# The scale of an expert weight in three VectorE operations, its squares' sum read as bfloat16 without a cast

## The chip, the cores and the metric

The kernel runs on one core of a Trainium2 chip. The metric is the time of one execution on the device in microseconds (us). Engine names are those of the profile: PE is TensorE's matmul and PEld its weight load, DVE is VectorE, ACT is ScalarE, POOL is GpSimd, SP is SyncE, which here only issues transfers.

## The reference

Three layers follow one another. Top-32 attention (2 batches, 8 heads, 576 rows, head size 64) makes 1152 rows of 512 values. A gated mixture layer with root-mean-square norm maps them to 1152 rows of 512. The last layer sends each row to one of eight experts and is the one that the change touches:

```python
logits = x @ w_gate                       # 1152 x 8
expert_idx = np.argmax(logits, axis=1)
# ... gate_w: softmax probability of the chosen expert; disp[e]: its rows, in order, up to 288
h = np.maximum(np.einsum('ecd,edf->ecf', disp, w1), 0.0)     # w1: 8 x 512 x 1024
y = np.einsum('ecf,efd->ecd', h, w2)                         # w2: 8 x 1024 x 512
out[i] = gate_w[i] * y[expert_idx[i], pos[i]]
```

## The kernel before

The 1152 rows are worked on as nine tiles of 128 (`NT` = 9, tile numbers 0 to 8). Attention and the gated layer fill the first three quarters of the span; the code writes their steps as generators that are advanced slot by slot, and the order of the instructions on each engine is then fixed by a planner that simulates the program and takes ready instructions by priority (`tc.high_priority(offset=...)` raises one). `after(...)` adds an edge: what stands in its block is not issued ahead of the instruction named. Each engine and each transfer queue works in the order so planned.

The experts' sixteen weight matrices (w1 and w2 of eight experts, 2 MB each, eight blocks of 128 x 512 fp32) are loaded one after the other in `ORDER`; n is the place in that order, j = 2e + w the matrix (w is 0 for w1, 1 for w2). A matrix isn't multiplied in fp32. It is scaled by a power of two and split into two fp16 halves, and `product` (L921) multiplies high by high, high by low and low by high, three matmuls for each 128 x 128 block. For each matrix:

- `load` (L773) issues two transfers on SP into a landing buffer; four buffers are used in turn, so a load waits for the conversion of an earlier matrix.
- `size` (L784) squares the matrix on ACT, in four pieces for n below 4 and in two later (L795); each piece leaves one sum per partition in a column of the small tile `sc`.
- `scale` (L800) casts these sums to bfloat16 on DVE (L804), adds them over partitions with matmuls against a matrix of ones (`st`, L806), and makes the power of two from the total on DVE: times 1.01 plus a tiny number (L807), shift right and mask (L809), times -1 plus a constant (L810), exponent alone (L148 in `exponent`), and the inverse of the power (L151 in `invert`). For w2 a further operation multiplies the two inverses of the expert (L816).
- `convert` (L818) writes the high half, one half of it on ACT (L825) and the other on DVE (L827), and the low half on DVE (L830).

`up` (L928) multiplies the gathered rows by w1 and applies the ReLU (high half on ACT L936, low half on DVE L937); `down` (L939) and `finish` (L976) multiply by w2 and take the scales out again on DVE (L945, L981, L994); `send` (L962) transposes back, multiplies by the gate on ACT (L973) and scatters the rows with POOL.

The first four matrices are sized and converted while the last tile (tile 8) still passes through the gated layer, and their DVE and ACT work is mixed with that tile's: its tanh (ACT L510), the products with it (DVE L511 and L514, which must be done before PE can transpose the result, L486), and the halves for the next matmul (ACT L470, DVE L471, then PE L531). After L531 the tile goes through `dispatch` (L540): router, slot, and a scatter by POOL (L621). Only then are rows gathered (L841, L854, L908), and behind these gathers SP issues the next weight loads.

```python
    with after(NT - 1, "sq"):
        size(0, 0)
        size(1, 1)
    with after(NT - 1, "xn"), after(NT - 1, "xn high"):
        convert(0, 0)
    size(2, 2)
    ...
    with tc.issue_after(last.ins):
        for _ in range(3):
            fetch_w()
```

A second copy of the program, for more than 168 rows of one expert (`exact`), is in the code behind a condition and isn't executed with these inputs.

Of the kernel before, what the change touches and what calls it, by code (L numbers as in the profile page):

```python
# [8 lines left out]
F32 = mybir.dt.float32  # L9
F32R = mybir.dt.float32r  # L10
F16 = mybir.dt.float16
BF16 = mybir.dt.bfloat16
I32 = mybir.dt.int32
U32 = mybir.dt.uint32
U8 = mybir.dt.uint8
AF = mybir.ActivationFunctionType
OP = mybir.AluOpType
PSUM = bass.MemoryType.PSUM

P = 128  # L20
# [19 lines left out]
TINY = 1e-24  # L40
# [22 lines left out]
def whole(  # L63
# [3 lines left out]
    nc = tc.nc  # L67
# [10 lines left out]
    ones16 = const.tile([P, P], BF16, name="ones16")  # L78
# [68 lines left out]
    def exponent(out, x):  # L147
        nc.vector.tensor_scalar(out.bitcast(I32), x.bitcast(I32), 0x7f800000, None, op0=OP.bitwise_and)  # L148

    def invert(out, x):  # L150
        nc.vector.tensor_scalar(out.bitcast(I32), x.bitcast(I32), -1, 0x7f000000, op0=OP.mult, op1=OP.add)  # L151
# [108 lines left out]
    raw = {}  # L260
# [47 lines left out]
    hi, lo = {}, {}  # L308
# [164 lines left out]
    yx, late, behind = {}, [], {}  # L473

    def after(*what):

        return tc.issue_after(behind[what].ins)
# [62 lines left out]
    def dispatch(t):  # L540
# [11 lines left out]
        nc.scalar.activation(sq.bitcast(BF16), y, AF.Square, accum_out=yn[:, 0:1])  # L552
        size = iter(()) if t == NT - 1 else pow2_below_rsqrt(yn[:, 1:2], yn[:, 2:3], yn[:, 0:1], 1.01, yn[:, 3:5])
        next(size, None)
        yield
        lp = px.tile([P, 3, E], F32, name="px")
# [138 lines left out]
    for p in range(NP):  # L695
        t, hp = divmod(p, 4)
# [11 lines left out]
    for t in range(NT):  # L708
        ew = nc.vector if t in (0, 8) else nc.gpsimd
# [35 lines left out]
    ew = ctx.enter_context(tc.tile_pool(name="ew", bufs=1, reuse_waits="tile"))  # L745
# [5 lines left out]
    es = {}  # L751
# [11 lines left out]
    def place(j):  # L763
        x = slots[slot_of[j]].bitcast(F16)
        return x[:, :8 * DM], x[:, 8 * DM:]

    def raw_of(n):

        if n < 2:
            return slots[2 + n]  # L770
        return raws[n % 2 if n < 4 else n % 4]
# [10 lines left out]
    BIG = 4 * DM  # L782

    def size(j, n):  # L784

        e, w = divmod(j, 2)
        raw = raw_of(n)
        sc = ew.tile([P, 13], F32, name="sc", bufs=8)
        k = 4 if n < 4 or exact else 2
        for g in range(k):  # L790
            if exact:
                junk = mx.tile([P, DM], F32, name="th").bitcast(BF16)
            else:
                junk = ew.tile([P, BIG], BF16, name="junk")[:, :2 * BIG // k]
            nc.scalar.activation(junk, raw[:, g * 2 * BIG // k:(g + 1) * 2 * BIG // k], AF.Square, accum_out=sc[:, 9 + g:10 + g])  # L795
        with tc.high_priority(offset=4000) if n < 4 and not exact else nullcontext():
            scale(e, w, n, k, sc)
        sized[j] = sc

    def scale(e, w, n, k, sc):  # L800

        t = sums_of[:, n % 8:n % 8 + 1]
        s16 = ew.tile([P, 4], BF16, name="s16", bufs=2)
        nc.vector.tensor_copy(s16[:, :k], sc[:, 9:9 + k])  # L804
        for g in range(k):
            nc.tensor.matmul(t[:, 0:1], ones16, s16[:, g:g + 1], start=(g == 0), stop=(g == k - 1))  # L806
        nc.vector.tensor_scalar(sc[:, 2:3], t[:, 0:1], 1.01, TINY, op0=OP.mult, op1=OP.add)  # L807
        half_bits = sc[:, 3:4].bitcast(I32)
        nc.vector.tensor_scalar(half_bits, sc[:, 2:3].bitcast(I32), 1, 0x7fff0000, op0=OP.logical_shift_right, op1=OP.bitwise_and)  # L809
        nc.vector.tensor_scalar(half_bits, half_bits, -1, 0x5f370000 + ((10, 14)[w] << 23), op0=OP.mult, op1=OP.add)  # L810
        exponent(sc[:, 7:8], sc[:, 3:4])
        invert(sc[:, 4:5], sc[:, 7:8])
        if w == 0:
            es[e] = sc
        else:
            nc.vector.tensor_tensor(es[e][:, 8:9], es[e][:, 4:5], sc[:, 4:5], op=OP.mult)  # L816

    def convert(j, n, high=True, low=range(4)):  # L818

        raw, (hi, lo), sc = raw_of(n), place(j), sized[j]  # L820
        k = 4 if n < 4 else 2
        for g in range(k) if high else ():
            r = slice(g * 2 * BIG // k, (g + 1) * 2 * BIG // k)
            if 2 * g < k:
                nc.scalar.activation(hi[:, r], raw[:, r], AF.Copy, scale=sc[:, 7:8])  # L825
            else:
                nc.vector.tensor_scalar(hi[:, r], raw[:, r], sc[:, 7:8], None, op0=OP.mult)  # L827
        for g in low[:k]:
            r = slice(g * 2 * BIG // k, (g + 1) * 2 * BIG // k)
            nc.vector.scalar_tensor_tensor(lo[:, r], raw[:, r], sc[:, 7:8], hi[:, r], op0=OP.mult, op1=OP.subtract)  # L830

    meta, every, xgT, hE, yT2 = {}, {}, {}, {}, {}
    had = route.tile([P, 1], F32, name="had", bufs=1)
# [23 lines left out]
    def chunks(n):  # L857
        return [(o, min(P, n - o)) for o in range(0, n, P)]
# [17 lines left out]
# [6 lines that stand above are left out]
    with after(NT - 1, "xn"):  # L882
        convert(1, 1, True, (0, 1))
    with after(NT - 1, "gs", 0):
        convert(1, 1, False, (2, 3))
# [29 lines left out]
    def groups(count, n):  # L915

        pieces = -(-count // (DM // n))
        g = -(-count // pieces)
        return [(c, min(c + g, count)) for c in range(0, count, g)]

    def product(a, w, x, nk, width, col, of=None):  # L921
        wh, wl = (y.rearrange("p (c f) -> p c f", f=width) for y in w)
        for c in of or range(nk):
            for n, (u, v) in enumerate(((wh, x[0]), (wh, x[1]), (wl, x[0]))):
                nc.tensor.matmul(a, u[:, c, col * P:(col + 1) * P], v[:, c, :a.shape[-1]],  # L925
                                 start=(c == 0 and n == 0), stop=(c == nk - 1 and n == 2))
# [12 lines left out]
    def down(k, e, n):  # L939
        yT2[k] = eb.tile([P, KC, n], F32, name="yT2", bufs=1)  # L940
        for lo, hi in groups(KC, n):
            a = pacc.tile([P, hi - lo, n], F32, name="acc")
            for c in range(lo, hi):
                product(a[:, c - lo, :], place(2 * e + 1), hE[k], NF2, DM, c)
            behind[k, "down"] = nc.vector.tensor_scalar(yT2[k][:, lo:hi, :], a, es[e][:, 8:9], None, op0=OP.mult)  # L945

    targets = {}

# [27 lines left out]
    def finish():  # L976
        k, x, cut, y = E - 1, KC - 1, NF2 - 3, eb.tile([P, KC, W], F32, name="yT2", bufs=1)
        a, z = (pacc.tile([P, w, W], F32, name="acc") for w in (x, 1))
        for c in range(x):
            product(a[:, c, :], place(2 * k + 1), hE[k], NF2, DM, c)  # L980
        nc.vector.tensor_scalar(y[:, :x, :], a, es[k][:, 8:9], None, op0=OP.mult)  # L981
        product(z[:, 0, :], place(2 * k + 1), hE[k], NF2, DM, x, range(cut))
        for i, (o, m) in enumerate(chunks(W)):
            ob, to = held[0].tile([P, DM], F32, name=f"last{i}"), held[0].tile([P, 1], I32, name=f"to{i}")
            with after("b", "down"):
                nc.vector.tensor_copy(to[:m], every[i][:m, k, 1:2])
            held.append((to[:m], ob[:m], False))
            tp = pback.tile([P, DM], F32, name="back")
            for c in range(x):
                last = nc.tensor.transpose(tp[:m, c * P:(c + 1) * P], y[:, c, o:o + m], ident)  # L990
            scaled(i, ob[:m, :x * P], tp[:m, :x * P], meta[k, i][:m, 0:1])
        with tc.issue_after(last.ins):
            product(z[:, 0, :], place(2 * k + 1), hE[k], NF2, DM, x, range(cut, NF2))
        nc.vector.tensor_scalar(y[:, x:, :], z, es[k][:, 8:9], None, op0=OP.mult)  # L994
        for i, (o, m) in enumerate(chunks(W)):
            tp = ptp.tile([P, P], F32, name="col")
            nc.tensor.transpose(tp[:m], y[:, x, o:o + m], ident)
            scaled(i, held[1 + i][1][:, x * P:], tp[:m], meta[k, i][:m, 0:1])

    def scaled(i, out, x, by):  # L1000
        if i:
            nc.vector.tensor_scalar(out, x, by, None, op0=OP.mult)
        else:
            nc.scalar.activation(out, x, AF.Copy, scale=by)
# [23 lines left out]
    def ready():  # L1028
# [11 lines left out]
        fetch_w()  # L1040

    down("a", 0, WA)
    up("b", 0, WB)
    ready()
    send("a", WA, True)
    up(1, 1, W)
    ready()
    down("b", 0, WB)
    ready()
    cnt = pback.tile([P, DM], F32, name="back")  # L1050
# [23 lines left out]
    if not exact:  # L1074
        finish()
        return nc.values_load(top[0:1, 0:1], min_val=0, max_val=2 * N), held, store
# [59 lines left out]
```

## Time and profile before

| what | value |
|---|---|
| time, three runs | 661.33, 662.97, 663.25 us; median 662.97 |
| the profiled execution's own time | 663.15 us, of which 661.2 us are the span |
| busy share of the span | PE 89%, PEld 62%, DVE 82%, ACT 76%, POOL 54% |
| granted TensorE clock, mean | 0.976 of full speed |
| chain that ended last, by engine | PE 52%, DVE 17%, ACT 9%, DMA 8%, POOL 6%, issue 6% |

All times inside the trace count from the start of the span. The share of the span is an average over very different stages, so what a change in one stage is worth is read from that stage: which engine has no idle time there, and which wait ends last. The profiled execution took 663.15 us, 0.18 us more than the median.

### The profile page before, as it was taken

The page shows a single profiled execution, that of the slowest core. Times are in us where ns is not written, and L with a number is a line of the kernel's source. Part 1 is how long each engine was busy: PE and PEld are TensorE (multiplying, and loading weights), DVE is VectorE, ACT ScalarE, POOL GpSimd, SP SyncE. Part 2 cuts the span into 40 slices and gives each one's busy share as a digit, 9 for nine tenths or more (in the row PEclk, how much of TensorE's full clock was granted, in tenths as well). Part 3 has the DMA queues.
Part 4 walks back from the last instruction along what each step waited for, and adds up shares of the span by engine and source line. Part 5 has one row for each costly group of instructions (what it writes and reads, how often), then busy time and mean ns, then how long its engine had stood idle before and what let it go on. Part 6 is the DMA issues. An engine that isn't in the chain of part 4 may idle for free.

```text
span 661.2 us, 13479 instructions
## 1 busy us (share of the span) xinstructions
PE 588.5 (89%) x4817; PEld 412.1 (62%) x4817; DVE 540.5 (82%) x1495; ACT 502.3 (76%) x972; POOL 353.8 (54%) x490
## 2 busy tenths in 40 slices
PE   1418879799999999999999999999998888999995
PEld 1314455545666666666666666665544688999995
DVE  3989999978989979989988999871379756999961
ACT  3459978997787878878897988875697539999721
POOL 2486644646468879958788688583212200123212
PEclk9999979799999999999999999999999898999998
DMA  8998355923000010100000000007600499999001
GB/s 217 271 327 292 142 183 181 303 85 83 20 16 25 18 45 9 33 17 29 14 13 30 17 26 0 1 17 266 245 17 34 142 213 395 309 355 359 28 22 43
DMA packets 47008, 80.07 MB, mean 121 GB/s; under 512 B 18717, under 2 KB 23325, under 8 KB 46931
## 3 DMA queue, kind: packets, MB, share of 16 engines
q1 hardware_dynamic: 45138, 74.28, 35.7%
q0 software_dynamic: 1792, 4.83, 2.0%
q8 instruction: 40, 0.66, 0.4%
q14 instruction: 38, 0.30, 0.1%
HBM read 64.35 MB, written 12.27 MB: 116 GB/s over the span
## 4 chain that ended last, share of the span: by engine, by line
PE 52%; DVE 17%; ACT 9%; DMA 8%; POOL 6%; issue 6%; SPq 1%; POOLq 0%; DVEq 0%; ACTq 0%
PE pm L502 15%; PE pm L531 9%; PE acc L925 7%; PE xps L430 6%; PE tp L317 5%; PE tp L422 4%; DVE split L830 3%; DMA vt<-in_v_l_dram 3%; DMA raw<-in_w_dram 3%; ACT junk L795 2%; DVE r L373 2%; DVE wbig L169 2%; DVE wbig L168 2%; PE pm L486 2%; DVE split L827 2%
## 5 line engine op out<-in xcount | busy, mean ns | idle before, releaser
L502 PE MATMUL pm<-wbig,xn 128*128 128x512 f16 x600 | 145.7, 379 | 0.5 <-DVE hT L471 0.5
L925 PEld LDWEIGHTS <-split 128*128 128x128 f16 x1728 | 116.4, 99 | 4.3 <-issue 2.0
L399 POOL TENSOR_TENSOR pp<-s,pp 128x576 f32<-128x576 f32 x72 | 101.9, 1431 | 21.8 <-ACT pp L398 21.5
L502 PEld LDWEIGHTS <-xn 128*128 128x128 f16 x648 | 62.3, 98 | 60.2 <-issue 0.9
L376 DVE MAX8 m<-r 128x8 f32<-128x288 f32 x216 | 96.5, 452 | 2.5
L373 DVE MATCH_REPLACE8 r<-m,r 128x288 f32<-128x288 f32 x216 | 95.1, 442 | 0.0
L317 PE MATMUL tp<-kst,qh 128*128 128x288 f32 (+1 forms) x160 | 64.9, 413 | 31.9 <-ACT s L319 14.6
L531 PE MATMUL pm<-wbig,hT 128*128 128x512 f16 x324 | 78.4, 386 | 0.0
L830 DVE SCALAR_TENSOR_TENSOR split<-raw,sc,split 128x2048 f16<-128x2048 f32 (+1 forms) x32 | 65.9, 2077 | 0.5 <-ACT split L825 0.5
L319 ACT ACTIVATE s<-tp 128x288 f32<-128x288 f32 x144 | 56.7, 416 | 11.1 <-PE tp L317 9.5
L423 ACT ACTIVATE pt<-tp 128x384 f32<-128x384 f32 x108 | 51.8, 499 | 15.2 <-PE tp L422 10.6
L317 PEld LDWEIGHTS tp<-kst,qh 128*128 128x128 f32 (+1 forms) x160 | 31.4, 197 | 50.5 <-ACT s L319 20.7
L422 PE MATMUL tp<-ident,pp 128*128 128x128 f32 x324 | 57.8, 288 | 5.3 <-DVE r L325 2.5
L430 PE MATMUL xps<-pt,vt 128*64 128x128 f32 (+1 forms) x800 | 62.4, 275 | 0.0
L925 PE MATMUL acc<-hE,split 128*128 128x168 f16 (+2 forms) x864 | 59.9, 231 | 1.7 <-DVE hE L937 1.7
L795 ACT ACTIVATE junk<-raw 128x2048 bf16<-128x2048 f32 (+1 forms) x32 | 54.1, 1692 | 6.9 <-DMA raw<-in_w_dram 6.7
L398 ACT ACTIVATE pp<-s,bias 128x576 f32<-128x576 f32 x72 | 52.2, 777 | 9.4 <-POOL bias L381 9.3
L404 ACT ACTIVATE pp<-pp,bias 128x576 f32<-128x576 f32 x72 | 57.0, 792 | 2.3 <-POOL pp L399 2.1
L925 PE MATMUL acc<-xgT,split 128*128 128x168 f16 (+1 forms) x768 | 58.0, 239 | 0.0
L422 PEld LDWEIGHTS tp<-ident,pp 128*128 128x128 f32 x324 | 40.5, 145 | 23.8 <-ACT pt L423 3.8
L430 PEld LDWEIGHTS xps<-pt,vt 128*64 128x64 f32 x800 | 43.9, 139 | 13.7 <-issue 12.0
L531 PEld LDWEIGHTS <-hT 128*128 128x128 f16 x324 | 30.4, 99 | 33.5 <-issue 2.7
(241 smaller groups left out, 1227.7 us busy)
## 6 DMA issues: line engine op xcount, KB each, us to landing
raw<-in_w_dram SPq DMA_DIRECT2D x28, 1024.0 KB, 7.4
wbig<-in_w_gate_dram SPq DMA_DIRECT2D x6, 1024.0 KB, 8.5
wbig<-in_w_val_dram SPq DMA_DIRECT2D x6, 1024.0 KB, 8.3
wraw<-in_w_out_dram SPq DMA_DIRECT2D x12, 512.0 KB, 5.8
disp<-wraw SPq DMA_DIRECT2D x18, 257.0 KB, 6.5
qraw<-in_q_l_dram SPq DMA_DIRECT2D x72, 64.0 KB, 2.2
wbig<-in_k_l_dram SPq DMA_DIRECT2D x16, 288.0 KB, 4.4
split<-in_w_dram SPq DMA_DIRECT2D x4, 1024.0 KB, 9.3
```

The lines of the kernel that those rows point to most:

```text
L317: nc.tensor.matmul(sp[:c1], x[:, i, :c1], kst[b, hp][:, i, c * HALF:(c + 1) * HALF], start=(n == 0), stop=(n == 1))
L373: nc.vector.match_replace(h[i], to[n - 1][:, i], h[i], -3.0e38)
L376: nc.vector.max(to[n][:, i], h[i])
L399: nc.gpsimd.tensor_tensor(w, s[i], w, op=OP.subtract)
L404: nc.scalar.activation(pp[p][:, i], pp[p][:, i], AF.Exp, bias=bias[:, i, 0:1], scale=0.125, accum_out=sums[t][:, h:h + 1])
L422: nc.tensor.transpose(tp[:, i, :], p2[:, o:o + P], ident)
L430: nc.tensor.matmul(xps[t][rows, hp, c0:c1], v, w, start=(n == 0), stop=(n == 4))
L502: behind[t, "prod", b] = nc.tensor.matmul(a, xn[:, x + c, :], half(i, lo), start=(c == 0 and n == 0), stop=(c == KC - 1 and n == 2))
L531: nc.tensor.matmul(yps, hT[f // KC][:, KC * hi + f % KC, :], half(i, lo), start=(f == 0 and n == 0), stop=(f == NF1 - 1 and n == 2))
L795: nc.scalar.activation(junk, raw[:, g * 2 * BIG // k:(g + 1) * 2 * BIG // k], AF.Square, accum_out=sc[:, 9 + g:10 + g])
L830: nc.vector.scalar_tensor_tensor(lo[:, r], raw[:, r], sc[:, 7:8], hi[:, r], op0=OP.mult, op1=OP.subtract)
L925: nc.tensor.matmul(a, u[:, c, col * P:(col + 1) * P], v[:, c, :a.shape[-1]], start=(c == 0 and n == 0), stop=(c == nk - 1 and n == 2))
```

## The change

`scale` no longer casts the sums and no longer multiplies by 1.01. The matmul against ones reads the upper 16 bits of each fp32 sum in place, through a bfloat16 view with a step of two. Three DVE operations follow: shift right by one and mask to the exponent (reading the matmul's result in PSUM as integers), times -1 plus a constant (the power of two, column 1), plus a constant (its inverse, column 2). The tile `sc` shrinks from 13 to 7 columns and `s16` is gone. The product of the two inverses is not formed; the operations that take the scales out again get both inverses as per-partition scalars and multiply twice.

```diff
-        sc = ew.tile([P, 13], F32, name="sc", bufs=8)
+        sc = ew.tile([P, 7], F32, name="sc", bufs=8)
...
-            nc.scalar.activation(junk, raw[:, ...], AF.Square, accum_out=sc[:, 9 + g:10 + g])
+            nc.scalar.activation(junk, raw[:, ...], AF.Square, accum_out=sc[:, 3 + g:4 + g])
...
         t = sums_of[:, n % 8:n % 8 + 1]
-        s16 = ew.tile([P, 4], BF16, name="s16", bufs=2)
-        nc.vector.tensor_copy(s16[:, :k], sc[:, 9:9 + k])
+        high = sc.bitcast(BF16).rearrange("p (c two) -> p c two", two=2)[:, :, 1]
         for g in range(k):
-            nc.tensor.matmul(t[:, 0:1], ones16, s16[:, g:g + 1], start=(g == 0), stop=(g == k - 1))
-        nc.vector.tensor_scalar(sc[:, 2:3], t[:, 0:1], 1.01, TINY, op0=OP.mult, op1=OP.add)
-        half_bits = sc[:, 3:4].bitcast(I32)
-        nc.vector.tensor_scalar(half_bits, sc[:, 2:3].bitcast(I32), 1, 0x7fff0000, op0=OP.logical_shift_right, op1=OP.bitwise_and)
-        nc.vector.tensor_scalar(half_bits, half_bits, -1, 0x5f370000 + ((10, 14)[w] << 23), op0=OP.mult, op1=OP.add)
-        exponent(sc[:, 7:8], sc[:, 3:4])
-        invert(sc[:, 4:5], sc[:, 7:8])
-        if w == 0:
-            es[e] = sc
-        else:
-            nc.vector.tensor_tensor(es[e][:, 8:9], es[e][:, 4:5], sc[:, 4:5], op=OP.mult)
+            nc.tensor.matmul(t[:, 0:1], ones16, high[:, 3 + g:4 + g], start=(g == 0), stop=(g == k - 1))
+        root, by, back = (sc[:, i:i + 1].bitcast(I32) for i in range(3))
+        c = (11, 15)[w]
+        nc.vector.tensor_scalar(root, t.bitcast(I32), 1, 0x7f800000, op0=OP.logical_shift_right, op1=OP.bitwise_and)
+        nc.vector.tensor_scalar(by, root, -1, (189 + c) << 23, op0=OP.mult, op1=OP.add)
+        nc.vector.tensor_scalar(back, root, (65 - c) << 23, None, op0=OP.add)
+        es.setdefault(e, []).append(sc[:, 2:3])
...
-                nc.scalar.activation(hi[:, r], raw[:, r], AF.Copy, scale=sc[:, 7:8])
+                nc.scalar.activation(hi[:, r], raw[:, r], AF.Copy, scale=sc[:, 1:2])
...
-            behind[k, "down"] = nc.vector.tensor_scalar(yT2[k][:, lo:hi, :], a, es[e][:, 8:9], None, op0=OP.mult)
+            behind[k, "down"] = nc.vector.tensor_scalar(yT2[k][:, lo:hi, :], a, es[e][-2], es[e][-1], op0=OP.mult, op1=OP.mult)
```

L827 and L830 take their scale from column 1 in the same way as L825, and L981 and L994 take two scalars in the same way as L945.

## Rows read from the trace of the kernel before

**Rows 1.** Stages of the span's end: busy us (instructions) per engine, clock, DMA share, GB/s
```profile
485.40:510.10 24.70, 21.72 (x127) 11.40 (x126) 23.87 (x50) 21.64 (x38) 4.42 (x7) 1.00 0.00 1
...
538.00:549.90 11.90, 8.96 (x184) 8.81 (x179) 1.33 (x4) 5.35 (x7) 1.03 (x1) 1.00 1.03 354
...
560.00:622.00 62.00, 62.00 (x848) 61.50 (x846) 59.56 (x99) 58.16 (x64) 13.81 (x7) 1.00 0.92 287
622.00:623.30 1.30, 0.07 (x2) 0.05 (x1) 1.30 (x4) 0.97 (x2) 0.72 (x1) 1.00 0.00 0
```

**Rows 2.** Operations on the tile sc: line, engine, count, min/median/max ns
```profile
L804 DVE CAST s<-sc x16: 149/160/303, 481.6 to 619.4; 128x2 bf16<-128x2 f32 x12, 128x4 bf16<-128x4 f32 x4
...
L816 DVE TENSOR_TENSOR sc<-sc x8: 146/150/213, 496.4 to 632.5; 128x1 f32<-128x1 f32 x8
```

**Rows 3.** DVE in order of time, 485 to 510: start, us, line, operation [idle before]
```profile
485.65 0.16 DVE L807 TENSOR_SCALAR sc<-st 128x1 f32<-128x1 f32 x1 [0.55 <-PE st L806]
...
486.62 0.17 DVE L804 CAST s<-sc 128x4 bf16<-128x4 f32 x1 [0.25 <-ACT junk L795]
...
487.00 1.42 DVE L827 TENSOR_SCALAR split<-split,sc 128x1024 f16<-128x1024 f32 x2
...
493.11 0.15 DVE L807 TENSOR_SCALAR sc<-st 128x1 f32<-128x1 f32 x1
...
496.40 0.15 DVE L816 TENSOR_TENSOR sc<-sc 128x1 f32<-128x1 f32 x1
...
503.42 0.14 DVE L561 COPY lg<-px 128x8 f32<-128x8 f32 x1
503.49 0.13 DVE L810 TENSOR_SCALAR sc<-sc 128x1 int32<-128x1 int32 x1
...
509.25 0.73 DVE L514 SCALAR_TENSOR_TENSOR gs<-late,st,th 128x512 f32<-128x512 f32 x1
```

**Rows 4.** DVE in order of time: two scale operations back to back
```profile
531.31 0.15 DVE L809 TENSOR_SCALAR sc<-sc 128x1 int32<-128x1 int32 x1
531.50 0.15 DVE L810 TENSOR_SCALAR sc<-sc 128x1 int32<-128x1 int32 x1
```

**Rows 5.** PE in order of time, 501 to 511
```profile
501.44 0.95 PE L558 MATMUL px<-rg,xu 128*128 128x8 f32 x8
...
510.04 0.72 PE L486 MATMUL pm<-ident,gs 128*128 128x128 f32 x4 [1.82 <-DVE gs L514]
510.55 8.31 PE L531 MATMUL pm<-wbig,hT 128*128 128x512 f16 x30
```

**Rows 6.** ACT and PE in order of time around 549
```profile
542.42 4.51 PE L925 MATMUL acc<-xgT,split 128*128 128x168 f16 x60
549.43 0.19 ACT L795 ACTIVATION_READ_ACCUMULATOR junk<-raw 128x1 f32 x1
549.87 0.19 PE L806 MATMUL st<-s,ones 128*128 128x1 bf16 x2 [2.94 <-DVE s L804]
```

**Rows 7.** Matmuls over bfloat16 values at a step of two (line L193)
```profile
L193 PE MATMUL tp<-wbig x144: 217/219/331, 23.9 to 116.3; 128*128 128x128 bf16 x144
```

**Rows 8.** DVE operations without and with two per-partition scalars, and the last scaling
```profile
L603 DVE TENSOR_SCALAR pos<-k x1: 146/146/146, 523.9 to 523.9; 128x1 f32<-128x1 f32 x1
...
L619 DVE TENSOR_SCALAR slot<-pos x1: 274/274/274, 524.7 to 524.7; 128x1 int32<-128x1 f32 x1
...
653.73 0.39 DVE L994 TENSOR_SCALAR yT<-acc,sc 128x168 f32<-128x168 f32 x1
```

**Rows 9.** Stages as in rows 1, around pauses of PE; then PE after one pause
```profile
510.00:514.00 4.00, 3.96 (x13) 1.74 (x14) 3.80 (x13) 2.71 (x3) 2.63 (x4) 0.57 0.69 262
...
538.00:540.00 2.00, 2.00 (x86) 2.00 (x82) 0.59 (x2) 0.00 (x0) 0.00 (x0) 1.00 1.13 207
...
550.00:555.00 5.00, 5.00 (x117) 4.98 (x115) 4.80 (x14) 5.00 (x7) 0.00 (x0) 0.66 1.04 418
...
537.74 2.60 PE L925 MATMUL acc<-xbT,split 128*128 128x48 f16 x96 [1.68 <-DMA xbT<-xb]
```

More of the change, by code (lines that the diff above doesn't have):

```diff
@@ L794, in size @@
                 junk = ew.tile([P, BIG], BF16, name="junk")[:, :2 * BIG // k]
-            nc.scalar.activation(junk, raw[:, g * 2 * BIG // k:(g + 1) * 2 * BIG // k], AF.Square, accum_out=sc[:, 9 + g:10 + g])
+            nc.scalar.activation(junk, raw[:, g * 2 * BIG // k:(g + 1) * 2 * BIG // k], AF.Square, accum_out=sc[:, 3 + g:4 + g])
         with tc.high_priority(offset=4000) if n < 4 and not exact else nullcontext():
@@ L824, in convert @@
             if 2 * g < k:
-                nc.scalar.activation(hi[:, r], raw[:, r], AF.Copy, scale=sc[:, 7:8])
+                nc.scalar.activation(hi[:, r], raw[:, r], AF.Copy, scale=sc[:, 1:2])
             else:
-                nc.vector.tensor_scalar(hi[:, r], raw[:, r], sc[:, 7:8], None, op0=OP.mult)
+                nc.vector.tensor_scalar(hi[:, r], raw[:, r], sc[:, 1:2], None, op0=OP.mult)
         for g in low[:k]:
             r = slice(g * 2 * BIG // k, (g + 1) * 2 * BIG // k)
-            nc.vector.scalar_tensor_tensor(lo[:, r], raw[:, r], sc[:, 7:8], hi[:, r], op0=OP.mult, op1=OP.subtract)
+            nc.vector.scalar_tensor_tensor(lo[:, r], raw[:, r], sc[:, 1:2], hi[:, r], op0=OP.mult, op1=OP.subtract)
     meta, every, xgT, hE, yT2 = {}, {}, {}, {}, {}
@@ L980, in finish @@
             product(a[:, c, :], place(2 * k + 1), hE[k], NF2, DM, c)
-        nc.vector.tensor_scalar(y[:, :x, :], a, es[k][:, 8:9], None, op0=OP.mult)
+        nc.vector.tensor_scalar(y[:, :x, :], a, es[k][-2], es[k][-1], op0=OP.mult, op1=OP.mult)
         product(z[:, 0, :], place(2 * k + 1), hE[k], NF2, DM, x, range(cut))
@@ L993, in finish @@
             product(z[:, 0, :], place(2 * k + 1), hE[k], NF2, DM, x, range(cut, NF2))
-        nc.vector.tensor_scalar(y[:, x:, :], z, es[k][:, 8:9], None, op0=OP.mult)
+        nc.vector.tensor_scalar(y[:, x:, :], z, es[k][-2], es[k][-1], op0=OP.mult, op1=OP.mult)
         for i, (o, m) in enumerate(chunks(W)):
```

## The prediction

> **What bounds the kernel now.** I read the shares of busy time first, then the stages of the last third, then the engines in order of time there. The shares name PE, but the stages differ. From 560 to 622 PE is busy for all 62.00 us, DVE for 59.56 and ACT for 58.16 [rows 1]: PE sets the pace, and a DVE operation saved there buys slack only. The one pause that DVE makes for PE is 1.23 us at 622 to 623.3 [rows 1]; DVE is there behind a conversion that itself waited for ACT, and ACT's work isn't changed. From 485.4 to 510.1 it is the other way round: DVE is busy 23.87 of 24.70 us and PE 21.72 [rows 1], and the stretch ends with PE waiting 1.82 us for DVE's L514 [rows 5]. What DVE gains there moves the last tile's L531, its router and scatter, the gathers behind the scatter and the weight loads that SP issues behind the gathers, so it should move the end by the same amount. The reader is to see that of 16 scalings only the first four lie in a stretch where DVE is late.
>
> **The change part by part.** Each scaling loses the cast and goes from five small operations to three; the eight of w2 lose L816 too [rows 2]: 16 x 3 + 8 = 56 operations of some 0.15 us. What one costs in time is its step to the next start. Behind one another, each on the one before, they start 0.19 us apart (531.31 to 531.50) [rows 4]; between other work the step is 0.07 (493.11 to 493.18, 503.42 to 503.49) [rows 3].
>
> The Trainium skill, page "VectorE: DVE Perf Modes", section "The DRAIN you can't avoid", says that eight copies take the same time with a semaphore after each as with one after the last, so that a wait between neighbours adds nothing. The trace doesn't agree: a dependent neighbour starts 0.12 us later than an independent one. By the rule every operation that goes from the stage would count 0.07, and the ten of them with a stall of 0.25 us would give 0.95 and a time of 661.9.
>
> First matrix: L807 starts at 485.65 when the matmul is done, and the conversion (L827) at 487.00 [rows 3]. Between them stand five small operations and the cast of the second matrix, which sits in DVE's queue until ACT has finished that matrix's squares (0.25 us idle) [rows 3]. Afterwards there is no cast to wait in, and the conversion follows three operations: 0.19 + 0.19 + 0.07 = 0.45 us in place of 1.35. Gain 0.90.
>
> Second matrix: seven small operations from 493.11 to 496.40 [rows 3], steps 0.07 + 0.19 + 0.06 + 0.12 + 0.19 + 0.07 + 0.07 = 0.77. Three stay, at 0.07 + 0.19 + 0.06. Gain 0.45, so 1.35 by 503.42.
>
> There a bound comes in. The copy of the router's logits (L561, 503.42) needs PE's L558, which ends at 501.44 + 0.95 = 502.39 [rows 5], and PE's order up to it has no pause. With 0.06 us from one engine to the other (as from L514's end, 509.25 + 0.73, to PE at 510.04 [rows 3, 5]) the copy can't start before 502.45, so only 0.97 of the 1.35 is kept. Third matrix: four more small operations from 503.49 on [rows 3], 0.30 us, of which about 0.12 stays: gain 0.18. So L514 at 509.25 [rows 3] moves by 1.15 us, and PE's wait with it. The fourth matrix's operations lie beside the 8.31 us of L531 [rows 5] and cost nothing; without that cover they would be worth what the third's six are, some 0.3.
>
> At 549.87 PE stood 2.94 us in front of the sum for a later matrix, of which the cast is the last part: ACT's sums were out at 549.43 + 0.19 = 549.62 [rows 6]. PE now waits for ACT itself and, with 0.06 us between engines, can go on at 549.68. If the matmul keeps its place, that is 0.19 gained; behind it in PE's queue stand 11 matmuls and then the next group, which ACT and DVE evict. If it is planned earlier by the cast's length, three matmuls of some 0.07 us (4.51 / 60 [rows 6]) land behind it and the gain is nothing; I take 0.19, since the plan's order is likelier to stay than to shift by exactly that. PE shows no pause at any other sum.
>
> Two costs. The second scalar: an operation with two takes 0.274 us against 0.146 with none [rows 8]; one scalar was there already, so the price is between 0 and 0.13, and I take 0.07. Of 16 such operations only L994 [rows 8] is on the path to the end, since PE has other matmuls beside the others: 0.07 lost. The matmul over a step of two: the row with such a step shows 128 columns at 0.219 us [rows 7], and two of the one-column sums take 0.19 together [rows 6]; between 0 and 0.05 each, I take 0, with up to 0.2 on the first matrix's path. The add that makes the inverse isn't in the trace; its neighbours' steps are 0.06 to 0.19, and only the lower end stands in front of a conversion.
>
> Sum: 1.15 + 0.19 - 0.07 = 1.27 us. The profiled execution's 663.15 becomes 661.88; it lies 0.18 above the median, so 661.7 is forecast for the median. Its own range, from the bounds above (gain 0.6 without the second and third terms kept, 2.0 if the logits come early too), is 661.0 to 662.4.
>
> **Rivals.** *The clock stays up.* From 485.4 on PE pauses 24.70 - 21.72 = 2.98 us [rows 1], 1.82 of it just before 510 [rows 5] and 1.16 in front of the transposes before those. They were followed by a granted clock of 0.57 from 510 to 514, in the middle of L531 [rows 9]: between its levels of 1.2 and 2.4 GHz, a loss of 0.43 x 4 = 1.7 us on the path. With DVE earlier the first pause vanishes and one of about 1.8 remains. For it: after a lone pause of 1.68 us [rows 9] the clock was 1.00 [rows 9]. Against it: 2.94 us alone brought 0.66 [rows 6, 9], and 1.8 lies between. Time 661.7 - 1.7 = 660.0.
>
> *Nothing moves.* The planner puts a conversion or an ACT step ahead of the last tile's instead, or the gain of the front is given back where PE and the loads run at 1.03 of the DMA engines' share from 538 [rows 1]. For it: ACT too is busy 21.64 of 24.70 us [rows 1], and the planned order is remade. Time 663.0.
>
> *Slower: the sum blocks PE.* Without the cast the matmul is ready sooner in the plan and may be put ahead of the 60 matmuls at 542.42 [rows 6]. PE then stands from 542.4 to 549.65 and does 60 x 0.074 = 4.4 us of work after the wait that it now does before. Each matmul passed costs 0.074; from 17 on, the 1.27 is gone. At 60 the time is 661.7 + 4.4 = 666.1. For it: PE has stood there already, so the plan expects the load sooner than it lands. Against it: the cast is only 0.17 us long.
>
> That the change doesn't do what it says hardly comes into question: the count of operations is fixed by the code.
>
> **How the numbers follow.** Forecast 0.40, clock kept 0.27, a larger gain from a better order 0.06, nothing 0.14, slower 0.13. A measurement of this kernel tells about 0.3% (2.0 us) from no change: faster means under 661.0, slower over 665.0. Faster: 0.25 of the second case, 0.06, and 0.08 from the lower end of the first: 0.39. Slower 0.12; the rest, 0.49, is the same. A range of 659.3 to 664.3 leaves out most of the slower and the larger cases.
>
> **What would show it.** In the profile after: no cast; the first matrix's L827 about 0.45 us after its first scale operation; the pause before the transposes of L514's last product (510.04) about 1.15 us earlier; SP's first weight load behind the gathers earlier by the same; PE full from 550 to 620 as before. The forecast is wrong if that transpose comes at 510 again, if PE waits longer for a sum, or if the clock after it differs from 0.57.

## The result and the profile after

The changed kernel took 654.51 us (median of 4 runs, 653.21 to 655.98) beside 662.46 for the kernel before: a ratio of 0.9884 [0.986, 0.9908]. Later (h0 below) it took 656.6 (6 runs, 654.61 to 658.75) beside 661.89: 0.9912 [0.9881, 0.9944]. So it is 5 to 8 us faster, and 661.7 with a range down to 659.3 was wrong.

The profiled execution took 654.35 us (span 652.4). The stage that answers to [rows 1] is a little shorter, and PE's stage without a pause is as full as before. Windows of the changed kernel (length, then busy time of PE, PE's loads, DVE, ACT and POOL with instruction counts, granted clock, DMA share, GB/s):

```profile
483.90:506.50 22.60, 21.66 (x123) 11.32 (x121) 22.25 (x40) 21.68 (x37) 3.04 (x6) 1.00 0.07 19
...
510.00:514.00 4.00, 3.59 (x17) 1.44 (x15) 4.00 (x6) 0.37 (x1) 0.89 (x1) 1.00 0.39 114
...
532.00:534.00 2.00, 1.94 (x49) 1.94 (x50) 0.00 (x0) 0.00 (x0) 0.00 (x0) 0.51 1.13 205
...
552.00:612.50 60.50, 60.50 (x832) 60.28 (x830) 60.09 (x76) 59.08 (x65) 14.56 (x7) 1.00 0.99 314
```

The stretch to the last transposes is 22.60 us long where it was 24.70, and the clock in the block behind it is 1.00 where it was 0.57 [rows 9]. It falls to 0.51 at 532 instead. DVE in the front of the changed kernel (start, length, operation, idle time before it), against [rows 3]:

```profile
483.46 0.15 DVE L808 TENSOR_SCALAR sc<-st 128x1 int32<-128x1 int32 x1
483.65 0.15 DVE L809 TENSOR_SCALAR sc<-sc 128x1 int32<-128x1 int32 x1
483.72 0.14 DVE L810 TENSOR_SCALAR sc<-sc 128x1 int32<-128x1 int32 x1
484.05 1.42 DVE L822 TENSOR_SCALAR split<-split,sc 128x1024 f16<-128x1024 f32 x2 [0.19 <-DVE sc L810]
485.38 4.87 DVE L825 SCALAR_TENSOR_TENSOR split<-split,sc,split 128x1024 f16<-128x1024 f32 x4
...
499.35 0.74 DVE L514 SCALAR_TENSOR_TENSOR x<-pm,st,th 128x512 f32<-128x512 f32 x1
500.01 1.41 DVE L822 TENSOR_SCALAR split<-raw,sc 128x1024 f16<-128x1024 f32 x2
501.33 1.28 DVE L825 SCALAR_TENSOR_TENSOR split<-raw,sc,split 128x1024 f16<-128x1024 f32 x1
502.53 0.16 DVE L561 COPY lg<-px 128x8 f32<-128x8 f32 x1
...
505.66 0.74 DVE L514 SCALAR_TENSOR_TENSOR gs<-late,st,th 128x512 f32<-128x512 f32 x1
```

And PE there, against [rows 5, 6]. The 1.16 us pause is gone, 1.82 is 0.64, and the 30 matmuls of L531 take 6.64 us where they took 8.31. The two pieces of n=5's sum are at 541.28 and 543.89, with 0.18 us of pause where there were 2.94:

```profile
506.46 0.66 PE L486 MATMUL pm<-ident,gs 128*128 128x128 f32 x4 [0.64 <-DVE nm L604]
506.95 6.64 PE L531 MATMUL pm<-wbig,hT 128*128 128x512 f16 x30
...
532.06 3.84 PE L920 MATMUL acc<-xbT,split 128*128 128x48 f16 x96 [2.98 <-DMA xbT<-xb]
...
541.28 0.17 PE L805 MATMUL st<-sc,ones 128*128 128x1 bf16 x1
...
543.89 0.16 PE L805 MATMUL st<-sc,ones 128*128 128x1 bf16 x1 [0.18 <-ACT junk L795]
```

The second scalar, by form (count, total us, mean ns): L940 takes 620 ns where L945 took 560 before, +0.06 us.

```profile
L945 DVE TENSOR_SCALAR yT<-acc,sc 128x336 f32<-128x336 f32 x12 | 6.7, 560 | 5.8 <-PE acc L925 5.8
...
L940 DVE TENSOR_SCALAR yT<-acc,sc 128x336 f32<-128x336 f32 x12 | 7.4, 620 | 5.8 <-PE acc L920 5.8
```

One warning about absolute times. Up to DVE's L514 of tile 7, at 478.78 before and 477.23 after, the two programs do the same work. That point lay between 476.40 (f4) and 484.57 (e1) in the profiles of this study, so 1.55 us of the first difference are no effect of the change. From here on, times are counted from it ("the anchor"). Both given kernels were profiled a second time (h0, h2), and the change was halved: k1 has the new scaling for the first four matrices alone, k2 for the other twelve alone.

| us from the anchor | before | before again | k2 | k1 | after | after again |
|---|---|---|---|---|---|---|
| last transposes of L514's products | 31.26 | 31.27 | 31.27 | 29.23 | 29.23 | 29.24 |
| yx of the last tile | 40.11 | 38.44 | 40.13 | 36.40 | 36.40 | 36.41 |
| last scatter | 47.10 | 45.99 | 47.10 | 43.69 | 43.76 | 43.69 |
| first weight load behind the gathers | 58.93 | 57.84 | 58.60 | 55.33 | 55.12 | 54.55 |
| last group of output transposes | 175.39 | 173.84 | 174.95 | 169.98 | 167.47 | 168.97 |

Taking the mean of two profiles for each kernel, the end comes 6.4 us sooner: 2.0 by the last transposes, 0.8 by yx (the clock: 1.7 in one pair, nothing in the other), nothing from there to the scatter, 0.7 from the scatter to the loads (11.84 to 11.11), and 2.8 from the loads to the end (116.23 to 113.39; in k1 114.65).

Where the last 2.8 us lie, PE's busy time shows. From the first load to the last transposes, in the kernel before, before again, after and after again (columns as above):

```profile
537.71:654.17 116.46, 111.78 (x1622) 110.72 (x1622) 90.48 (x156) 83.18 (x92) 20.60 (x14) 0.99 0.71 233
...
536.29:652.29 116.00, 111.78 (x1622) 110.52 (x1618) 89.67 (x153) 83.30 (x92) 23.92 (x14) 0.99 0.71 234
...
532.35:644.70 112.35, 111.27 (x1620) 110.34 (x1616) 87.09 (x114) 82.49 (x92) 23.80 (x14) 0.99 0.73 242
...
533.79:648.21 114.42, 111.82 (x1622) 110.91 (x1622) 87.75 (x116) 82.62 (x92) 24.86 (x14) 0.99 0.72 237
```

PE is busy for 111 to 112 us in all four. It stands idle for 4.7 and 4.2 us before, for 1.1 and 2.6 after: 2.6 of the 2.8 us. Most of it is two waits. One is n=5's sum (2.94 and 2.53 us before, 0.18 and 1.94 after). The other is a later wait for the halves hE that DVE makes (L937): 1.23 us before, 0.39 and 0.82 in the second profile. Behind n=5's sum neither profile of the changed kernel has a wait of 0.2 us or more for hE. PE before and before again:

```profile
623.25 2.92 PE L925 MATMUL acc<-hE,split 128*128 128x168 f16 x38 [1.23 <-DVE hE L937]
...
621.32 2.92 PE L925 MATMUL acc<-hE,split 128*128 128x168 f16 x38 [0.82 <-DVE hE L937]
```

### The profile page after: what moved, and what is told of

Read it like the earlier page. It is cut to its first block, busy times and chain, and to the rows that moved or that the text cites. A ratio compares the mean times of both kernels' runs of the same rounds, so it can differ in the third digit from the quotient of the medians.

```text
span 652.4 us, 13434 instructions
## 1 busy us (share of the span) xinstructions
PE 583.8 (89%) x4817; PEld 409.2 (63%) x4817; DVE 533.5 (82%) x1439; ACT 501.6 (77%) x972; POOL 355.6 (55%) x490
## 4 chain that ended last, share of the span: by engine, by line
PE 61%; DMA 10%; DVE 9%; ACT 8%; POOL 6%; issue 3%; SPq 2%; POOLq 0%; DVEq 0%; ACTq 0%
PE pm L502 16%; PE acc L920 15%; PE pm L531 9%; PE xps L430 6%; PE tp L317 5%; PE tp L422 4%; ACT junk L795 3%; DMA disp<-wraw 2%; DMA wbig<-in_k_l_dram 2%; DVE r L373 2%; PE pm L486 2%; POOL pp L399 1%; DVE wbig L168 1%; DMA raw<-in_w_dram 1%; DVE wbig L169 1%
## 5 line engine op out<-in xcount | busy, mean ns | idle before, releaser
L920 PEld LDWEIGHTS <-split 128*128 128x128 f16 x1728 | 114.8, 99 | 5.1 <-DMA xbT<-xb 3.2
L531 PE MATMUL pm<-wbig,hT 128*128 128x512 f16 x324 | 76.7, 380 | 0.0
L825 DVE SCALAR_TENSOR_TENSOR split<-raw,sc,split 128x2048 f16<-128x2048 f32 (+1 forms) x32 | 65.9, 2076 | 0.1
L920 PE MATMUL acc<-xgT,split 128*128 128x168 f16 (+1 forms) x768 | 56.4, 234 | 0.4 <-issue 0.4
L531 PEld LDWEIGHTS <-hT 128*128 128x128 f16 x324 | 29.8, 98 | 32.0 <-issue 1.0
```

Source lines behind the costliest of these rows:

```text
L531: nc.tensor.matmul(yps, hT[f // KC][:, KC * hi + f % KC, :], half(i, lo), start=(f == 0 and n == 0), stop=(f == NF1 - 1 and n == 2))
L825: nc.vector.scalar_tensor_tensor(lo[:, r], raw[:, r], sc[:, 1:2], hi[:, r], op0=OP.mult, op1=OP.subtract)
```

## The experiments

Four theories were tested. A: the cast's absence alone does it, since the cast held all pieces of a sum back until the last square was done. B: it is the number of DVE's small operations. C: it is where the planner puts the last piece of a sum in PE's order, against the landing of its load. P: POOL's small steps stand still while DVE converts, and the scatter of the last tile but one comes late. Times of *before* beside the runs are 661.9 to 662.7.

**The halves of the change.** k1 takes the new `scale` for experts 0 and 1 (n<4), k2 for the others; in both, L945 and its like take one or two scalars as the expert has them.

```
+        if e < 2 and not exact:      # k2: e >= 2
+            ...the three operations, no cast
+            return
         ...the old scale
```

> The new scaling for the first four matrices (n<4) alone, the old one for the other twelve. The last tile's last transposes come 2.0 us sooner behind the anchor L514 (29.2 in place of 31.26). If the parts add: 660 (662.0 - 2.0), with a pause for n=5's sum as before of 2 to 3 us. If the front's gain is lost on the way to the end, as in f5_cast_front: 662 to 664.

> The old scaling for the first four matrices, the new one for the other twelve. The transposes stay at 31.26 behind the anchor. If the parts add, the rest of the gain, 655.6 - 660.0 = -4.4: 657.5 to 658. If the gain behind the front needs the front as well: 660 to 662, as f4_no_cast_late (660.0), which lacks only the cast there. n=5's last piece is at 2903 in PE's order, 29 matmuls ahead of the changed kernel's 2932, so theory C expects pauses of 1 to 2 us there.

k1: 658.27 (656.02 to 663.09), ratio 0.994 [0.9916, 0.9964]. k2: 661.92 (659.1 to 664.15), 0.9999 [0.9977, 1.0021]. The parts don't add: the front alone gives 4.0 us, twice what it was expected to, the rest alone gives nothing, and both give 5 to 8. k1's PE (start, length, operation, pause before it):

```profile
508.81 0.66 PE L486 MATMUL pm<-ident,gs 128*128 128x128 f32 x4 [0.64 <-DVE nm L604]
509.31 6.64 PE L531 MATMUL pm<-wbig,hT 128*128 128x512 f16 x30
...
547.33 0.19 PE L817 MATMUL st<-s,ones 128*128 128x1 bf16 x2 [0.33 <-DVE s L815]
```

k1 still has the cast in front of n=5's sum, and the pause there is 0.33 us all the same: in the re-made plan this sum is 29 matmuls later in PE's order than in the kernel before. In k2 it is 4 sooner, and PE waits 3.5 us in two pieces without any cast:

```profile
509.62 1.00 PE L486 MATMUL pm<-ident,gs 128*128 128x128 f32 x4 [1.83 <-DVE gs L514]
510.42 8.02 PE L531 MATMUL pm<-wbig,hT 128*128 128x512 f16 x30
...
545.40 0.16 PE L806 MATMUL st<-sc,ones 128*128 128x1 bf16 x1 [2.13 <-ACT junk L795]
...
549.45 0.16 PE L806 MATMUL st<-sc,ones 128*128 128x1 bf16 x1 [1.33 <-ACT junk L795]
```

**Both kernels again** (no edit).

> The changed kernel again, on the chip of the runs beside it. If 654.5 was typical: 654 to 656, and in its profile the last tile's L531 block and yx at full clock again. If the clock or the first 477 us of that execution were luck: 656 to 658.5.

> The kernel before again, one look. If the granted clock's fall in the last tile's L531 block follows from the pauses of 1.16 and 1.82 us before it, the fall is there again (L514's transposes to yx some 8.8 us); if not, 7.2 us, as in f4_no_cast_late with the same pauses.

h0: 656.6, told above, in the range that was expected if the first 654.5 was in part luck; h2: 661.31, one run. In h0 the order is the changed kernel's own, and still PE waits 1.94 us for n=5's second piece, where the first profile has 0.18. PE came there sooner (the first piece's matmul is at 62.68 from the anchor, in the first profile at 64.05): its clock was 1.00 all the way from 532 to 546, and not 0.51 at 532. PE in h0:

```profile
546.29 0.16 PE L805 MATMUL st<-sc,ones 128*128 128x1 bf16 x1 [1.94 <-ACT junk L795]
```

Neither has the fall of the clock in the L531 block. In h2 the granted clock fell earlier, where PE had time to spare: it reached the transposes later and the 1.82 us pause in front of them was gone. A window of h2 (columns as above), then its PE:

```profile
504.00:506.00 2.00, 2.00 (x6) 0.72 (x5) 2.00 (x6) 2.00 (x3) 0.75 (x2) 0.50 0.00 0
```

```profile
503.22 0.74 PE L486 MATMUL pm<-ident,x 128*128 128x128 f32 x4 [1.16 <-DVE x L514]
...
509.72 0.66 PE L486 MATMUL pm<-ident,gs 128*128 128x128 f32 x4
510.21 6.64 PE L531 MATMUL pm<-wbig,hT 128*128 128x512 f16 x30
...
547.81 0.19 PE L806 MATMUL st<-s,ones 128*128 128x1 bf16 x2 [2.53 <-DVE s L804]
```

**The cast.** e1: the kernel before, without the cast alone.

```
-        nc.vector.tensor_copy(s16[:, :k], sc[:, 9:9 + k])
+        s16 = sc.bitcast(BF16).rearrange("p (c two) -> p c two", two=2)[:, 9:, 1]
```

> The kernel before with the cast alone removed: the matmuls against ones read the upper halves of the fp32 sums in place, each as soon as its own piece is squared; the five small operations and L816 stay. Theory A (the cast, one operation over all pieces, held every partial sum until the last piece was squared, and PE with it): most of the 8.0 us go, 654 to 657.5 us. Theory B (what counts is the number of small DVE operations, 16 of the 56 removed here): 662.5 - 8.0 x 16/56 = 660.2 us.

661.2 (658.28 to 666.97), 0.9975 [0.9954, 0.9996]. A's time is missed; B's 660.2 lies inside the interval. The front says more than the time. DVE's anchor, then PE:

```profile
484.57 0.75 DVE L514 SCALAR_TENSOR_TENSOR gs<-pm,st,th 128x512 f32<-128x512 f32 x1 [1.23 <-PE px L599]
...
513.21 0.66 PE L486 MATMUL pm<-ident,gs 128*128 128x128 f32 x4 [0.15 <-DVE gs L514]
...
527.12 2.72 PE L924 MATMUL acc<-xgT,split 128*128 128x128 f16 x24 [2.79 <-DMA xgT<-disp]
529.63 0.21 PE L598 MATMUL px<-oh,before 128*128 128x8 bf16 x1
```

The last transposes come at 28.64 from the anchor, sooner than in the changed kernel (29.23), though the five small operations are all there. The gain is lost on the way to the scatter, which comes at 46.88, as late as before (47.10 and 45.99): PE's order has the products with the gathered tokens ahead of the last tile's router matmul L598, and PE waits 2.79 us for the tokens. L598 so comes at 45.06 from the anchor, in the changed kernel at 41.26.

e2: the kernel before, the cast in k single casts, each in front of its matmul.

```
         for g in range(k):
+            nc.vector.tensor_copy(s16[:, g:g + 1], sc[:, 9 + g:10 + g])
```

> The kernel before with the cast cut into one cast per piece: 40 casts in place of 16, so 24 more small DVE operations, but each partial sum goes to PE by itself. Theory A: faster than before nearly as the kernel without casts, 655 to 658.5 us. Theory B: slower than before by some 24 x 0.07 to 0.19 us where DVE is late, 662.5 to 665 us.

660.63 (657.1 to 662.7), 0.9972 [0.9953, 0.9992]; transposes at 31.27. More small operations and no tie gave 1.9 us, of which the clock in the L531 block was 1.7 in the profiled run. The time lies between A's range and B's.

f4: the kernel before, cast left out for n>=4 alone.

```
+        if n < 4:
             nc.vector.tensor_copy(s16[:, :k], sc[:, 9:9 + k])
+        else:
+            s16 = sc.bitcast(BF16).rearrange("p (c two) -> p c two", two=2)[:, 9:, 1]
```

> The kernel before with the cast removed for the twelve later matrices (n from 4) and kept for the first four, so that the front, up to the last tile's scatter, stays as it was. The last piece of the sixth matrix stands at 2903 in PE's order (2907 in the kernel before). Theory A: the 2.94 us pause goes, 659 to 660.5 us. Theory C: a pause of 2 to 3 us stays at that matmul, 661.5 to 663.5 us.

660.01 (658.08 to 662.17), 0.9971 [0.9956, 0.9987]. The time is as A said, the pauses at n=5 (1.25 and 0.78 us) as C said. Its pauses before the transposes were 1.16 and 1.82 us, as before, and the clock didn't fall in the block behind them. PE in f4:

```profile
501.17 0.66 PE L486 MATMUL pm<-ident,x 128*128 128x128 f32 x4 [1.16 <-DVE x L514]
...
507.66 0.65 PE L486 MATMUL pm<-ident,gs 128*128 128x128 f32 x4 [1.82 <-DVE gs L514]
508.15 6.64 PE L531 MATMUL pm<-wbig,hT 128*128 128x512 f16 x30
```

f4 and e1 differ by the cast of the first four matrices alone: with it the transposes come at 31.26 from the anchor, without it at 28.64.

e3: the changed kernel with one cast over all pieces; f5: the same for n<4 alone.

```
+        s16 = ew.tile([P, 4], BF16, name="s16", bufs=2)
+        nc.vector.tensor_copy(s16[:, :k], sc[:, 3:3 + k])    # f5: under if n < 4
```

> The changed kernel with one cast over all pieces put back: 40 of the 56 operations are gone, the pieces are tied together again. Theory A: only the shorter chain is gained, some 1 to 2 us: 660 to 662 us, with PE's pause in front of a sum at about 547 to 550 back. Theory B: 662.5 - 8.0 x 40/56 = 656.8 us.

> The changed kernel with the cast put back for the first four matrices alone. If the shorter chain of DVE operations makes the gain of the front, tile 8's last transposes come as early as in the changed kernel (about 29.2 us behind the last L514 of tile 7, in the kernel before 31.3) and L531 runs at the full clock. In this plan the reciprocal of tile 7's softmax stands behind two conversions on DVE, as in the kernel with the cast kept everywhere; if that is what delayed the gather there, PE waits some 3 us for the gathered rows again: 658 to 664 us. If the cast in the front costs nothing and the placing neither: 654 to 656 us.

e3: 668.2 (666.54 to 669.54), 1.0084 [1.0057, 1.0112], slower than the kernel before. f5: 663.23 (662.25 to 666.39), 1.0016 [1.0001, 1.0031]. e3 is above both of its ranges, f5 inside its slower one. In both the transposes come at 29.1, as in the changed kernel, so the three operations bring the front's 2.0 us with the cast still there, as e1 brings them by the cast's absence alone. Either edit does it, and the two don't add; what each of them moves in the plan was not taken apart. All of the gain, and more, is then lost, first as in e1: PE waits for tokens that are gathered behind the scatter of the last tile but one, with L598 behind that wait (f5):

```profile
520.49 1.87 PE L923 MATMUL acc<-xgT,split 128*128 128x128 f16 x16 [3.00 <-DMA xgT<-disp]
522.15 0.21 PE L598 MATMUL px<-oh,before 128*128 128x8 bf16 x1
```

**The place of the sum.** e4: the changed kernel, each sum's matmuls in the opposite order, so that all wait for the last piece. f1: the same for n=5 alone, the rest of the plan being unchanged.

```
-        for g in range(k):
+        for g in reversed(range(k)):       # f1: only if n == 5
```

> The changed kernel with the matmuls of one total in the opposite order: the one that opens the accumulation is that of the last piece, so all of them wait until the last piece is squared, as behind the cast, but no operation is added on any engine. Theory A: much of the gain is lost, 657.5 to 661.5 us. Theory B: as the changed kernel, 654 to 655.5 us.

> The changed kernel with the two matmuls of one total alone in the opposite order, that of the sixth matrix (n = 5), where the kernel before stood 2.94 us. Only this pair moves in PE's order: both stand where the later one stood (matmuls 2931 and 2932 in PE's order, in the changed kernel 2891 and 2932, in the kernel before 2906 and 2907). Theory A (a total whose pieces are tied holds PE): 1 to 2.9 us slower than the changed kernel, 655.5 to 657.5 us. Theory C (what counts is where the last piece's matmul stands in PE's order against the time at which its load lands): as the changed kernel, 653.5 to 655.5 us, with no pause above 0.3 us there.

e4: 660.51 (658.0 to 667.73), 0.9975 [0.9949, 1.0], inside A's range, transposes at 30.35. f1: 655.61 (653.6 to 660.65), 0.9907 [0.9877, 0.9936], where A's range and C's meet; its profile has no pause over 0.3 us at n=5, as C said. Tying this one pair costs nothing that shows where the plan stays. Tying them all re-makes the plan, so e4 doesn't tell the tie from the order.

g1: the changed kernel, with the last products of up(1) and those of down("b") behind n=5's sum. Its last piece is then 24 matmuls sooner.

```
+                with after("sum", 5) if k == 1 and c == NF2 - 1 else ...:
+                with after("sum", 5) if k == "b" else nullcontext():
```

> The changed kernel; the last twelve products of up(1) and those of down("b") are ordered behind the first later sum's last piece (n=5), which so comes 24 matmuls sooner on PE. Theory C (25 matmuls passed hide the wait for that load): PE pauses there again, by up to 24 x 0.07 = 1.7 us, and the time is 655.5 to 657.5, above the changed kernel's 654.5. Theory A (the cast's absence alone removes the pause): no pause, 654 to 655.

659.15 (655.97 to 660.66), 0.9942 [0.992, 0.9965], above both ranges. Three pauses came: 0.52 us in front of n=5's last piece, 0.80 in front of a later sum's and 0.51 for hE; from the anchor the end is at 169.67, 1.4 behind the mean of the changed kernel's two profiles (168.22). h0 has 1.94 us at n=5 without this edit, so g1's 0.52 is no proof of C.

```profile
546.58 0.16 PE L805 MATMUL st<-sc,ones 128*128 128x1 bf16 x1 [0.52 <-ACT junk L795]
...
553.48 0.16 PE L805 MATMUL st<-sc,ones 128*128 128x1 bf16 x1 [0.80 <-ACT junk L795]
554.15 2.92 PE L920 MATMUL acc<-xgT,split 128*128 128x168 f16 x38 [0.51 <-DVE hE L932]
```

v1 fills the 2.98 us pause at 532 with other products; v3 also puts n=5's sum behind up("b").

```
-    up("b", 0, WB)        ...        up(1, 1, W)
+    up(1, 1, W)           ...        up("b", 0, WB)
+            with after("b", "made") if n == 5 and not exact else nullcontext():    # v3
```

> The changed kernel with the up products of expert 1 emitted ahead of those of the gathered expert's b half. In the changed kernel PE stands 2.98 us for the gathered tokens at 532.06 and then runs at a granted clock of 0.51 for 2 us. If these products fill the pause: 650.5 to 653.5. If they can't start there, since their weights aren't scaled yet: 654 to 655.5; over 656 if the new order gives a later wait.

> v1_up1_first (659.9) with n=5's sum behind the b half's up products. Theory C: v1's pauses of 2.80 and 1.01 us in front of that sum shrink to under 1 in all, and the time falls below the changed kernel's by up to the 2.98 us pause for the gathered tokens that is filled now: 652 to 654.5. If the loads that follow the gathers set the end, pauses only move: 654.5 to 657.

v1: 659.88 (655.11 to 662.1), 0.9952 [0.9929, 0.9976]; v3: 659.46 (657.47 to 662.4), 0.9964 [0.9942, 0.9986]. v3 is above both of its ranges, and neither beats the changed kernel. In v1 the pause for the tokens is gone and comes back in front of the sum:

```profile
543.93 0.16 PE L805 MATMUL st<-sc,ones 128*128 128x1 bf16 x1 [2.80 <-ACT junk L795]
...
547.34 0.16 PE L805 MATMUL st<-sc,ones 128*128 128x1 bf16 x1 [1.01 <-ACT junk L795]
```

v3 has 1.88 us there. PE gets work earlier, but the sum waits for ACT's squares of a matrix whose load starts when the gathers are out (54.84 from the anchor in v3): what is filled at 532 is lacking at 545.

**POOL beside DVE's conversions.** f6: f5 with the second pair of the third matrix's low conversions behind the reciprocal of the last tile but one.

```
-    with after(NT - 1, "dve"):
+    with after(NT - 1, "dve"), after(NT - 2, "recip"):
         convert(2, 2, False, (2, 3))
```

> The kernel before this one in the list (changed kernel, cast in the front) with one edge added: the two conversions may not be issued ahead of tile 7's reciprocal. If the reciprocal's place costs what the traces say, PE's wait for the gathered rows goes and the time is 2.5 to 3.5 us below that kernel's; if not, it is the same as that kernel's within 0.7 us.

665.82 (665.49 to 667.16), 1.0059 [1.0045, 1.0074]: missed. The reciprocal came sooner, and then a POOL step of 0.27 us (L610 in the changed kernel) took 2.32. DVE, POOL and PE in the timeline of f6:

```profile
510.98 2.46 DVE L828 SCALAR_TENSOR_TENSOR split<-raw,sc,split 128x1024 f16<-128x1024 f32 x2
...
511.18 2.32 POOL L610 TENSOR_SCALAR yd<-nm,yn 128x1 f32<-128x1 f32 x1
...
522.54 2.61 PE L923 MATMUL acc<-xgT,split 128*128 128x128 f16 x23 [3.40 <-DMA xgT<-disp]
```

It ends at 513.50, just as DVE's pair does (513.44). g2: f5 with that tile's slot steps on DVE and the second pair of conversions behind them.

```
-        ev = nc.vector if t == NT - 1 else nc.gpsimd
+        ev = nc.vector if t >= NT - 2 else nc.gpsimd
```

> f5_cast_front (663.2) with the small slot operations of the last tile but one on DVE in place of POOL, and DVE's second matrix's low conversions behind them. Theory P (POOL's small operations are held while DVE converts, so that tile's scatter and its gather come late): its scatter comes 1 to 2.5 us sooner, PE's wait of 3.0 us for that gather shrinks below 1 us, and the time is 660 to 661.5. If the late gather has another cause: 662.5 to 664.

663.89 (662.12 to 666.67), 1.0025 [1.0003, 1.0047]: inside the range for another cause than P, and the wait for the tokens grew. But now it is the scatter's own issue on POOL, 1.10 us in the changed kernel, that takes 4.94 beside four conversions. DVE, POOL and PE in the timeline of g2:

```profile
512.74 4.88 DVE L828 SCALAR_TENSOR_TENSOR split<-raw,sc,split 128x1024 f16<-128x1024 f32 x4
...
513.63 4.94 POOL L621 DMA_INDIRECT disp<-yd,slot  x1 [5.44 <-DVE slot L619]
...
524.02 2.61 PE L923 MATMUL acc<-xgT,split 128*128 128x128 f16 x23 [4.86 <-DMA xgT<-disp]
```

h1: f5 with these conversions behind the scatter's issue.

```
+            with tc.issue_after(scat[-1].ins):
+                nc.gpsimd.memset(gone[:, 0:1], 0.0)
+            behind[t, "gone"] = nc.vector.tensor_copy(gone[:, 1:2], gone[:, 0:1])
```

> f5_cast_front (663.2), with DVE's second pair of low conversions of the third matrix put behind the scatter of the last tile but one (through a small memset on POOL and a copy on DVE). Theory P (POOL's steps and its scatter stand still while DVE does these two-input conversions): that scatter comes some 3 us sooner than f5's (35.3 us behind the anchor L514), PE's 3.00 us wait for the gathered tokens goes, and the time is 660 to 661.5. If the late gather isn't due to POOL standing still: 663 or more, since DVE now waits as well.

664.33 (661.28 to 667.84), 1.0026 [1.0001, 1.0051]. The time is that of the other half, 663 or more, but the first half held in the trace: the scatter took 1.25 us, came at 33.0 in place of 35.3, and PE's wait shrank from 3.00 to 1.65. The time didn't follow: PE then waited 1.61 for the last tile's router, and the end, at 175.9 from the anchor, is where f5 has it (175.76). So DVE's conversions do make that scatter late. How much of it is POOL standing still, and how much the reciprocal that DVE does behind them, wasn't told apart, and neither settles what f5 loses.

**One more small operation.** f3: a spare [128,1] memset in each scaling, PE's order as in the changed kernel.

```
+        nc.vector.memset(ew.tile([P, 1], F32, name="spare", bufs=2), 0.0)
```

> The changed kernel with one spare [128,1] memset on DVE in each of the 16 scalings, PE's order being the same. If time follows the number of DVE's small operations (theory B): the four of the front cost 4 x 0.06 to 0.19 us, 0.2 to 0.8, so 654.8 to 655.4. If it follows the order alone (theory C): 654.3 to 654.8.

658.0 (656.15 to 659.53), 0.9927 [0.9898, 0.9956], above both expectations; but its profile (658.57) has the anchor at 480.87, and from there the end is at 168.18, between the changed kernel's two. In that profile no cost of B's shows; what is over lies ahead of the first scaling. It is one profile.

## Why the prediction was wrong

**The front, 1.15 forecast, 2.03 measured.** The right stage, undersized. The first matrix's conversion follows its first scale operation by 0.59 us (0.45 forecast, 1.35 before). That operation itself is also 0.64 earlier from the anchor, which the sum left out; in e1, with the cast alone gone, it is as early. The second and third matrices give the rest, 0.63, as forecast ahead of the bound. The bound at the logits' copy L561 was the wrong step here. PE's L558 did stay where it was (22.66 us from the anchor before, 22.69 after), but nothing forces the conversion behind the copy to wait for it: the new plan puts 2.5 us of the third matrix's conversion (from 500.01 on) ahead of the copy, at 502.53, so the front kept the whole gain. That the gain comes of fewer operations in a chain, as the sum has it, is not shown: e1 has the whole of it with five.

**The clock, held as a rival at 0.27, came true in the measured run,** which was in part luck. It is not a term of the plan alone. With the front as it was, the L531 stretch from the transposes to yx took 8.85 us in two profiles (before, k2) and 7.17 in two (h2, f4), with the 1.16 and 1.82 us pauses in f4 and k2 as in the kernel before. With the three operations in the front it took 7.17 to 7.20 in thirteen of fourteen profiles, and 8.86 in e4. So the row [rows 9] on which the forecast kept its 1.7 was one outcome of two, and by these four and fourteen profiles the change takes an average of 0.7 away, an estimate.

**The step that failed** is the one that valued what lies behind the loads. It took two terms there. For n=5's sum: "I take 0.19, since the plan's order is likelier to stay than to shift by exactly that", with "PE full from 550 to 620 as before". It left the 1.23 us pause at 622 as it was, since "ACT's work isn't changed". From the first load to the end the change gave 2.8 us, not 0.19 less 0.07, and 2.6 of it is idle time of PE. The order didn't stay: n=5's last piece moved 25 matmuls later in PE's order (2907 to 2932), and the pause of 2.94 (2.53 in h2) is 0.18 (1.94 in h0). The pause at 622 went too, in both profiles. The forecast saw the shift of the order as a mechanism, priced it at 0.074 us per matmul passed, and let it work only in the bad direction (its slower rival). At that price 25 matmuls make 1.85 us, an estimate beside the 1.7 by which the pause shrank on the mean of two profiles. That the place in the order alone does it is not shown: k1 has the shift, the cast and a short pause, but h0 has the shift and a long one. Why the pause at 622 went stays open.

**The second scalar:** +0.06 per operation (0.07 forecast), right. **56 operations fewer,** right: DVE has 1439 instructions, before 1495. **"It should move the end by the same amount":** wrong. The front's 2.0 became 4.0 (k1), 0 or less (f5, e3).

**Open:** why the planner's order gains behind the loads with both halves of the change and less with one; why k2 gains nothing where f4, which changes less of the same twelve scalings, gains 1.9 (in the profiled runs 1.7 of the 2.2 us between them are the clock in the L531 block); and why f5 and e3 lose 7 to 13 us against the changed kernel with the same front. In f5's profile 2.6 of 7.5 us are gone by the last scatter and 4.7 go between the loads and the end, where PE stands idle for 7.1 us. Late scatter, pauses at n=5 (1.55 and 1.15) and waits of PE for hE are all seen there; no run took them apart.

## What to carry to other kernels

Where a planner makes the order anew, an edit's own price is the smaller half: parts of this one, alone or recombined, gave 654.5 to 668.2 us, so forecast with a range as wide as the order's known waits (here one of 2.9 us) in both directions. Take a stretch's clock and the time up to a common point from at least two executions before a term rests on them. When a small POOL step or a scatter is on the path, look at what DVE does beside it.

## What the runs showed of the hardware

POOL stands still beside DVE's conversions with two inputs from SBUF: in f6 a 0.27 us step took 2.32, to the end of DVE's pair, and in g2 the issue of a scatter took 4.94 in place of 1.10, to 0.95 us behind the end of DVE's four. It isn't always the whole run: in f5 a POOL step of 0.38 us (L619) took 1.45 and was over behind the first of two. The Trainium skill, page "SBUF — State Buffer", section "Who interferes with whom", says that a DVE instruction with two SBUF inputs contends with a GpSimd instruction that reads SBUF; the trace of f6 agrees (2.32 us). In the kernel before, the scatter's issue at 512.24 takes 2.05.

The granted clock fell at different places of the same program: 510 to 514 in one execution of the kernel before, 504 to 506 in the other, where it cost nothing, since PE waited for DVE there anyway. And the stretch up to the anchor, all but the same code in every kernel, took 476.40 to 484.57 us: 8.2 us apart, more than most of the effects measured here.
